# Batches 0 and 1 by head pair: early q and k on the sync queue, transposes on TensorE up front, weights in order on the GpSimd queue

## The chip, the cores and the metric

The kernel runs on one core of a Trainium2 chip. A core has TensorE (PE, with its weight loads PEld), VectorE (DVE), ScalarE (ACT), GpSimd (POOL) and SyncE (SP); each works through its own instructions in their order and waits on semaphores for the others. The metric is the device time of one execution in microseconds (us). The kernel before took 326.36 us, the median of three runs (324.55, 326.36 and 326.54).

## The reference

```python
# q, k, v: (8, 8, 576, 64) float32;  beacon_k, beacon_v: (8, 8, 16, 64)
k_all = concatenate([beacon_k, k], axis=2)
v_all = concatenate([beacon_v, v], axis=2)
scores = matmul(q, k_all.transpose(0, 1, 3, 2)) / sqrt(64)
scores = where(causal, -1e9, scores)          # beacons are always seen, tokens causally
a = softmax(scores)
x = matmul(a, v_all).transpose(0, 2, 1, 3).reshape(4608, 512)
a, b = x @ w1, x @ w2                         # w1, w2: (512, 1024)
out = ((a * b) @ w3) @ w_out                  # w3: (1024, 1024), w_out: (1024, 512)
```

The kernel folds `w3 @ w_out` into one matrix `Wt` (1024 x 512) on the chip and then computes `(a * b) @ Wt`. Inputs and output are float32; all matmuls take float16.

## The kernel before

**Attention.** A batch has eight steps `s`, two for each of the four head pairs `t`. A step is `scores(s)` (matmuls of `kT` and `qT` into two PSUM tiles `ps`, L344), `exps(s, 0)` and `exps(s, 1)` (ACT, L353, into `pT`), `mask(s, j)` (DVE, L365, times the triangles `MA` and `MB`), `values(s)` (matmuls of `pT` and `va` into `pv`, L382), and then a reciprocal and a product on DVE that write `x16` (L390, L391). `va` holds v for one batch in five chunks of 128 keys (beacons first, so the last chunk has 80 rows), with a column of ones for the softmax's sum. `va`, `q16`, `k16`, `qT` and `kT` exist twice; batch `b` uses number `b % 2`. `ps` has two buffers, `pv` one.

**Operands.** `load_q`, `load_k` and `load_v` are DMAs of the GpSimd queue that cast float32 to float16, a chunk of 128 tokens and all heads at a time, in pieces of 64 elements. For batches 0 and 1, `pe_transpose_qk` turns a chunk of q and k by eight TensorE transposes (L210) and two copies out of PSUM (L211 on DVE, L212 on ACT). From batch 2 on, DMA transposes on the sync queue do it (L125, L126).

**Weights.** `w_out` and `w3` come in float32 over the sync queue into staging tiles `st` and are cast by ACT and DVE (`cast`, L150 and L152) into `wo16` and `w3c`. `w1` and `w2` come by casting DMAs of the GpSimd queue into `w12`, behind batch 0's q, k and v (L196).

**The stream of matrix work.** `stream()` yields one matmul of 512 columns at a time. First come the 64 units of `fuse` (L255, each row block of `w3` is first turned by `w3_transposed`, L232, and copied by DVE, L234), then, for each 512 tokens `mc`, 64 units of `ff_ab` (L277) and 32 of `ff_out` (L298). `emit_ff(n)` places the next `n` units between the attention's instructions; `fill[s]` says how many go to step `s`. The order is written out by hand (`manual_schedule`); the framework only adds the semaphore waits which the tiles' reads and writes call for, also between two writes of the same place.

**The start.** TensorE is given 16 units of `fuse`, then batch 0's five chunks of transposes with 8 units behind each of the first four, then `scores(0)` and the steps 0 to 7 with ten units of `fuse`. At `s == 7` come the last six units of `fuse`, `pe_transpose_x(0)` (batch 0's x into `xT`), then 45 units of `ff_ab` between batch 1's five chunks of transposes and three more, then batch 1's steps with 38 units, then `pe_transpose_x(1)`. From batch 2 on (`s >= 16`) a step has 11 or 12 units.

Of the kernel before, what the change touches and what calls it, by code (L numbers as in the profile page):

```python
# [39 lines left out]
def kernel(  # L40
# [21 lines left out]
    NKT = DM // P  # L62
    NFT = DF // P
    NJT = 5
    NB2 = 2
    VS = 72
    scale = float(D**-0.5)
# [17 lines left out]
    sm = ctx.enter_context(tc.tile_pool(name="sm", bufs=4))  # L85
    gp = ctx.enter_context(tc.tile_pool(name="gp", bufs=2))
    wp = ctx.enter_context(tc.tile_pool(name="wp", bufs=2))
    wc = ctx.enter_context(tc.tile_pool(name="wc", bufs=3))
    stg = ctx.enter_context(tc.tile_pool(name="stg", bufs=5))
    asb = ctx.enter_context(tc.tile_pool(name="asb", bufs=3))  # L90
    op = ctx.enter_context(tc.tile_pool(name="op", bufs=4))
    psS = ctx.enter_context(tc.tile_pool(name="psS", bufs=2, space=bass.MemoryType.PSUM))
    psV = ctx.enter_context(tc.tile_pool(name="psV", bufs=1, space=bass.MemoryType.PSUM))
    psM = ctx.enter_context(tc.tile_pool(name="psM", bufs=3, space=bass.MemoryType.PSUM))
# [4 lines left out]
    def load_q(b, c):  # L99
        rows = min(P, S - c * P)  # L100
        nc.gpsimd.dma_start(  # L101
            q16s[b % NB2][:rows, c, :].rearrange("s (h d) -> s h d", h=H),
            q[b, :, ds(c * P, rows), :].rearrange("h s d -> s h d"),
        )
# [11 lines left out]
    def load_k(b, jt):  # L116
        load_kv(b, jt, k, beacon_k, k16s[b % NB2][:, jt, :].rearrange("s (h d) -> s h d", h=H))

    def load_v(b, jt):
        load_kv(b, jt, v, beacon_v, vas[b % NB2][:, jt, :, 0:64])  # L120
# [5 lines left out]
        nc.sync.dma_start_transpose(kTs[i][:, :, ds(c * P, P)], k16s[i][:, c, :])  # L126


    def stage(src):
        st = stg.tile([P, 2 * DM], FP32, name="st")  # L130
        if len(src.shape) == 3:
            nc.sync.dma_start(st.rearrange("p (c n) -> p c n", c=2), src)
        else:
            nc.sync.dma_start(st, src)
        return st

    wo_v = moe_w_out.rearrange("(a c p) n -> a p c n", p=P, c=2)
    srcs = [moe_w3[ts(0, P), :]] + [wo_v[a] for a in range(4)]
    srcs += [moe_w3[ts(kt, P), :] for kt in range(1, NFT)]
    staged = [stage(srcs.pop(0)) for _ in range(5)]  # L140
    w3c = {}

    def cast(engine, row=None, piece=None):
        st = staged.pop(0)
        if row is None:
            dst = wo16[:, ds(2 * piece, 2), :].rearrange("p c n -> p (c n)")
        else:
            w3c[row] = dst = wc.tile([P, 2 * DM], FP16, name="w3c")
        if engine is nc.scalar:
            nc.scalar.copy(dst, st)  # L150
        else:
            nc.vector.tensor_copy(dst, st)  # L152
        if srcs:
            staged.append(stage(srcs.pop(0)))

    nc.vector.memset(ident, 1.0)
    nc.gpsimd.affine_select(
        ident,
        ident,
# [3 lines left out]
        base=0,  # L163
        channel_multiplier=-1,
    )

    for i in range(NB2):
        nc.vector.memset(k16s[i][64:128, 4, :], 0.0)
        nc.vector.memset(vas[i][64:128, 4, :, :], 0.0)
        nc.vector.memset(q16s[i][64:128, 4, :], 0.0)  # L170

    for c in range(NJT):
        load_q(0, c)
        load_k(0, c)
    nc.vector.memset(MA, 1.0)
    nc.vector.memset(MB, 1.0)
    for m, base in (
        (MA[:, 0:128], 0),
        (MA[:, 128:240], Nb),
# [11 lines left out]
        )  # L191
    for c in range(NJT):
        load_v(0, c)
    for c in range(4):
        for i, w in enumerate((moe_w1, moe_w2)):
            nc.gpsimd.dma_start(  # L196
                w12[:, :, ds(i * DF + c * 256, 256)],
                w[:, ts(c, 256)].rearrange("(t p) f -> p t f", p=P),
            )
    for c in range(NJT):  # L200
        load_q(1, c)
        load_k(1, c)


    def pe_transpose_qk(b, c):
        i = b % NB2
        pt = psM.tile([P, 2, NT, P], FP16, name="pm")
        for j, d16 in enumerate((q16s[i], k16s[i])):
            for t in range(NT):
                nc.tensor.transpose(pt[:, j, t, :], d16[:, c, ts(t, P)], ident)  # L210
        nc.vector.tensor_copy(qTs[i][:, :, ts(c, P)], pt[:, 0])  # L211
        nc.scalar.copy(kTs[i][:, :, ts(c, P)], pt[:, 1])  # L212

    def pe_transpose_x(b):
        for i in range(NJT):
            pt = psM.tile([P, NT, P], FP16, name="pm")
            n = QTN[i]
            for t in range(NT):
                nc.tensor.transpose(
                    pt[:, t, 0:n], x16s[b][:n, i, ts(t, P)], ident[:n, :n]  # L220
                )
            dst = xT[:, :, ds(b * S + QT0[i], n)]
            if i % 2:
                nc.scalar.copy(dst, pt[:, :, 0:n])  # L224
            else:
                nc.vector.tensor_copy(dst, pt[:, :, 0:n])


    def w3_transposed(kt):
        pt = psM.tile([P, NFT, P], FP16, name="pm")  # L230
        for rt in range(NFT):
            nc.tensor.transpose(pt[:, rt, :], w3c[kt][:, ts(rt, P)], ident)  # L232
        wT = wp.tile([P, NFT, P], FP16, name="wT")
        nc.vector.tensor_copy(wT, pt)  # L234
        return wT

    cast(nc.scalar, row=0)
    cast(nc.vector, piece=0)
    cast(nc.scalar, piece=1)
    nc.vector.memset(vas[0][:, 0:4, :, 64:65], 1.0)  # L240
    nc.vector.memset(vas[0][0:80, 4, :, 64:65], 1.0)
    cast(nc.vector, piece=2)
    cast(nc.scalar, piece=3)
    cast(nc.vector, row=1)
    nc.vector.memset(vas[1][:, 0:4, :, 64:65], 1.0)
    nc.vector.memset(vas[1][0:80, 4, :, 64:65], 1.0)


    def fuse():
        wT = w3_transposed(0)  # L250
        for kt in range(NFT):
            nxt = w3_transposed(kt + 1) if kt + 1 < NFT else None
            pm = psM.tile([P, DM], FP32, name="pm")
            for rt in range(NFT):
                nc.tensor.matmul(  # L255
                    pm,
                    wT[:, rt, :],
                    wo16[:, rt, :],
                    start=(rt == 0),
                    stop=(rt == NFT - 1),  # L260
                )
                if rt == 0 and kt + 2 < NFT:
                    cast((nc.scalar, nc.vector)[kt % 2], row=kt + 2)
                if rt < NFT - 1:
                    yield
            nc.scalar.copy(Wt[:, kt, :], pm)
            wT = nxt
            yield
# [81 lines left out]
    def exps(s, j):  # L350
        g = 2 * (s % 2) + j
        pT = pTs[s // 2]
        nc.scalar.activation(  # L353
            pT[:, :, ds(GO[g], GW[g])], pss[s][j][:, :, 0 : GW[g]], AF.Exp, scale=scale
        )
# [50 lines left out]
    NSB = 2 * NT  # L406
    NS = B * NSB
    LEFT = 50
    n_second = 38
    n_kept = 10  # L410
    n_first = 96 - n_second - n_kept
    fill = [0] * NS
    fill[0:7] = [2, 2, 2, 1, 1, 1, 1]
    for s in range(NSB, 2 * NSB):
        fill[s] = n_second * (s - NSB + 1) // NSB - n_second * (s - NSB) // NSB
    rest, n = n_kept + 6 * 96 - LEFT, NS - 2 * NSB
    for s in range(2 * NSB, NS):
        fill[s] = rest * (s - 2 * NSB + 1) // n - rest * (s - 2 * NSB) // n

    emit_ff(16)  # L420
    for c in range(NJT):
        pe_transpose_qk(0, c)
        if c < NJT - 1:
            emit_ff(8)
    for c in range(NJT):
        load_v(1, c)
    for c in range(NJT):
        load_q(2, c)
        load_k(2, c)
    scores(0)  # L430
    for j in range(2):
        exps(0, j)
        mask(0, j)
    for s in range(NS):
        b, r = s // NSB, s % NSB
        if s == NSB - 1:
            values(s)
            emit_ff(64 - emitted)
            pe_transpose_x(0)
            for c in range(NJT):  # L440
                emit_ff(n_first // NJT)
                pe_transpose_qk(1, c)
            emit_ff(64 + n_first - emitted)
            scores(s + 1)
            for j in range(2):
                exps(s + 1, j)
                mask(s + 1, j)
            continue
        if s + 1 < NS:
            scores(s + 1)  # L450
            exps(s + 1, 0)
        values(s)
# [50 lines left out]
```

The softmax here doesn't subtract the row's maximum and nothing guards it: scores larger than these inputs give would overflow.

## Time and profile before

| | |
|---|---|
| median of three runs | 326.36 us |
| the profiled execution's own time | 326.37 us |
| its span, first to last instruction | 324.5 us |
| mean granted TensorE clock | 0.995 |
| busy PE / DVE / ACT / POOL | 286.7 / 161.5 / 163.9 / 117.2 us |
| GpSimd's DMA queue (q0) | 119040 packets, 16.52 MB |
| sync's DMA queue (q1) | 53312 packets, 26.75 MB |
| read from HBM, written to it | 39.32 MB, 9.44 MB |

The span ends with TensorE's last matmuls, so what counts in it is the time in which TensorE has nothing to do. Read the table of groups for the duration of one instruction of each kind, the timeline for the times at which stages begin, and the windows for the load of each engine and the bytes per second of a stage. The bytes of a casting DMA are counted as float16, as they land; its source is twice as large. A bracket at the end of a timeline's row is the engine's idle time before it and what ended it.

### The profile page before, as it was taken

To read this page: it belongs to the slowest core of one execution; us is meant where nothing else is said; L and a number is where in the kernel's file an instruction comes from. 1 tells how busy PE (TensorE), PEld (TensorE's weight loads), DVE (VectorE), ACT (ScalarE), POOL (GpSimd) and SP (SyncE) were. 2 spreads that over 40 slices of the span, in tenths; PEclk is the share of its full clock that TensorE was granted. 3 is DMA by queue.
4 is the path that set the end of the run, shared out by engine and by line. 5 is a ranking of instruction groups with operands and counts; after the bars stand their busy time and mean duration, and the time that the engine had idled before them with its cause. 6 is when DMAs were issued, how large, how long until landed. Compare 5 with 4: busy or idle time off the path is not lost.

```text
span 324.5 us, 6919 instructions
## 1 busy us (share of the span) xinstructions
PE 286.7 (88%) x2776; PEld 148.2 (46%) x2776; DVE 161.5 (50%) x375; ACT 163.9 (51%) x229; POOL 117.2 (36%) x153
## 2 busy tenths in 40 slices
PE   1179777987999999999999999799999989999995
PEld 0135445543455445444554455354445544444442
DVE  3324454453664655555654655465555653343342
ACT  2325785467656665655466557464764452230320
POOL 8029869975178019505820960230000000000000
PEclk9997999999999999999999999999999999999999
DMA  8999999999999979999999999996551132202103
GB/s 242 342 288 126 167 175 146 138 144 145 119 113 187 140 86 155 208 138 126 180 176 162 138 206 175 95 146 178 68 84 65 67 32 61 111 2 91 38 2 129
DMA packets 172384, 43.72 MB, mean 135 GB/s; under 512 B 161600, under 2 KB 165696, under 8 KB 172352
## 3 DMA queue, kind: packets, MB, share of 16 engines
q0 software_dynamic: 119040, 16.52, 78.5%
q1 hardware_dynamic: 53312, 26.75, 41.7%
q8 instruction: 22, 0.36, 0.5%
q14 instruction: 10, 0.08, 0.1%
HBM read 39.32 MB, written 9.44 MB: 150 GB/s over the span
## 4 chain that ended last, share of the span: by engine, by line
PE 69%; DMA 12%; ACT 6%; DVE 5%; issue 3%; POOL 3%; DVEq 0%; ACTq 0%; POOLq 0%
PE pm L277 31%; PE pm L298 17%; PE pv L382 10%; PE ps L344 6%; DMA k<-in_beacon_k_dram 6%; ACT pT L353 5%; DMA k<-in_k_dram 3%; PE pm L255 3%; DMA qT<-q 3%; PE pm L210 1%; DVE pT L365 1%; DVE gT L290 1%; DVE x L391 1%; POOL q L101 1%; ACT a_sb L288 1%
## 5 line engine op out<-in xcount | busy, mean ns | idle before, releaser
L277 PE MATMUL pm<-xT,w 128*128 128x512 f16 x576 | 132.8, 379 | 0.6 <-ACT xT L224 0.5
L353 ACT ACTIVATE pT<-ps 128x736 f16<-128x736 f32 (+3 forms) x128 | 105.8, 863 | 35.3 <-PE ps L344 34.5
L288 ACT ACTIVATE a_sb<-pm 128x512 f32<-128x512 f32 x72 | 43.0, 597 | 81.2 <-PE pm L277 80.3
L277 PEld LDWEIGHTS <-w 128*128 128x128 f16 x576 | 53.6, 98 | 58.7 <-issue 0.9
L290 DVE TENSOR_TENSOR gT<-pm,a_sb 128x512 f16<-128x512 f32 x72 | 49.7, 690 | 47.2 <-PE pm L277 43.4
L298 PE MATMUL pm<-Wt,gT 128*128 128x512 f16 x288 | 66.7, 379 | 0.0
L110 POOL DMA_DIRECT2D va<-in_v_dram x40 | 34.0, 871 | 69.2 <-PE pv L382 68.1
L344 PE MATMUL ps<-qT,kT 64*128 64x80 f16 (+3 forms) x704 | 38.3, 228 | 13.0 <-ACT pT L353 9.8
L382 PE MATMUL pv<-va,pT 128*128 128x65 f16 x960 | 41.0, 194 | 3.4 <-DVE pT L365 2.4
L344 PEld LDWEIGHTS <-kT 64*128 64x128 f16 x704 | 20.9, 94 | 42.9 <-issue 41.2
L298 PEld LDWEIGHTS <-gT 128*128 128x128 f16 x288 | 26.9, 98 | 29.6 <-DVE gT L290 0.2
L110 POOL DMA_DIRECT2D k<-in_k_dram x40 | 34.8, 871 | 15.1 <-DMA q<-in_q_dram 10.7
L390 DVE RECIPROCAL rd<-pv 128x4 f32<-128x4 f32 x64 | 12.1, 189 | 55.0 <-PE pv L382 54.9
L101 POOL DMA_DIRECT2D q<-in_q_dram x40 | 35.5, 888 | 10.3 <-DMA k<-in_beacon_k_dram 6.1
L382 PEld LDWEIGHTS <-pT 128*128 128x128 f16 x960 | 33.0, 97 | 13.4 <-DVE pT L365 7.6
L308 DVE TENSOR_SCALAR ot<-pm 128x512 f32<-128x512 f32 x36 | 24.8, 689 | 20.9 <-PE pm L298 20.7
L391 DVE TENSOR_TENSOR x<-pv,rd 128x256 f16<-128x256 f32 x64 | 31.4, 491 | 2.4
L365 DVE TENSOR_TENSOR pT<-pT,MB 128x512 f16<-128x512 f16 x64 | 19.3, 324 | 6.4 <-ACT pT L353 6.4
L255 PE MATMUL pm<-wo,wT 128*128 128x512 f16 x64 | 18.3, 420 | 0.0
L232 PE MATMUL pm<-ident,w3c 128*128 128x128 f16 x64 | 5.8, 243 | 13.6 <-DVE w3c L152 8.3
L365 DVE TENSOR_TENSOR pT<-pT,MA 128x480 f16<-128x480 f16 x32 | 12.7, 398 | 1.8 <-ACT pT L353 1.8
L232 PEld LDWEIGHTS <-w3c 128*128 128x128 f16 x64 | 4.6, 110 | 14.1 <-DVE w3c L152 8.6
(38 smaller groups left out, 82.8 us busy)
## 6 DMA issues: line engine op xcount, KB each, us to landing
out_dram<-ot SPq DMA_DIRECT2D x36, 256.0 KB, 2.4
st<-in_moe_w_dram SPq DMA_DIRECT2D x8, 512.0 KB, 6.7
q<-in_q_dram POOLq DMA_DIRECT2D x32, 128.0 KB, 8.7
k<-in_k_dram POOLq DMA_DIRECT2D x24, 128.0 KB, 9.6
va<-in_v_dram POOLq DMA_DIRECT2D x24, 128.0 KB, 5.5
st<-in_moe_w_out_dram SPq DMA_DIRECT2D x4, 512.0 KB, 7.7
w<-in_moe_w_dram POOLq DMA_DIRECT2D x8, 256.0 KB, 7.9
k<-in_k_dram POOLq DMA_DIRECT2D x8, 112.0 KB, 7.8
```

The lines of the kernel that those rows point to most:

```text
L101: nc.gpsimd.dma_start(q16s[b % NB2][:rows, c, :].rearrange("s (h d) -> s h d", h=H), q[b, :, ds(c * P, rows), :].rearrange("h s d -> s h d"),)
L110: nc.gpsimd.dma_start(dst[ds(p0, rows)], src[b, :, ds(s0, rows), :].rearrange("h s d -> s h d"))
L255: nc.tensor.matmul(pm, wT[:, rt, :], wo16[:, rt, :], start=(rt == 0), stop=(rt == NFT - 1),)
L277: nc.tensor.matmul(pm, w12[:, kt, ds(i * DF + kf * P, P)], xT[:, kt, ds(mc * 512, 512)], start=(kt == 0), stop=(kt == NKT - 1),)
L288: nc.scalar.activation(a_sb, pm, AF.Copy, scale=GS)
L290: nc.vector.tensor_tensor(gT[:, kf, :], pm, a_sb, ALU.mult)
L298: nc.tensor.matmul(pm, gT[:, kf, ts(mt, P)], Wt[:, kf, :], start=(kf == 0), stop=(kf == NFT - 1),)
L344: nc.tensor.matmul(ps[:, hh, ds(col, n)], kT[ds(hh * 64, 64), t, ts(jt, P)], qT[ds(hh * 64, 64), t, ds(q0, n)],)
L353: nc.scalar.activation(pT[:, :, ds(GO[g], GW[g])], pss[s][j][:, :, 0 : GW[g]], AF.Exp, scale=scale)
L365: nc.vector.tensor_tensor(blk, blk, m.unsqueeze(1).to_broadcast([P, 2, n]), ALU.mult)
L382: nc.tensor.matmul(pv[:, 2 * n + hh, 0:65], pT[:, hh, ds(col, P)], va[:, jt, 2 * t + hh, 0:65], start=(jn == 0), stop=(jn == len(BLK[i]) - 1),
L391: nc.vector.tensor_tensor(x16[:, ds(tiles[0], ni), ds(t * P, P)].rearrange("p i (h d) -> p i h d", h=2), pv[:, 0 : 2 * ni, 0:64].rearrange ...
```

## The change

It concerns what happens before batch 2; the code of batches 2 to 7 stays. The pool of `a_sb` goes from three buffers to two, that of `ot` from four to three, and the staging pools `stg` and `wc` go away.

- q and k of batches 0 and 1 are loaded by head pair (`load_pair`), in float32, in runs of six tokens, which are 1536 contiguous bytes: partition `p` holds tokens 6p to 6p+5 of two heads. Batch 0's come over the sync queue, batch 1's over the GpSimd queue. `cast_pair` casts a pair on DVE, `pe_transpose_pair` turns it with 13 transposes (six for q, six for k, one for the beacons) and copies it to `qT` (DVE) and `kT` (ACT), with columns at a distance of six.
- `w_out` and `w3` come by casting DMAs on the GpSimd queue, behind batch 0's v and ahead of `w1` and `w2`; `w3` is kept in a part of `xT` that is written late. The casts on ACT and DVE go.
- Attention comes first: the pairs of batch 0, with `scores(0)`, its exps and its masks between them, and steps 0 to 6 without stream units, but eight at step 6. At `s == 7` come 16 units, `pe_transpose_x(0)`, the other 40 of `fuse`, then 28 units of `ff_ab` (before: 48) between batch 1's four pairs; batch 1's steps have 58 (before: 38).
- `constants(i)` gathers the memsets of `kT`'s unused columns and of `va`'s chunk 4 (rows 64 to 127 to zero) and ones. `constants(0)` stands at the start. `constants(1)` and the memsets of `k16` and `q16` stand behind batch 0's last pair and behind the lines that issue batch 1's loads of v; before, these stood at the start.

```diff
+    def load_pair(b, t):
+        engine = nc.gpsimd if b else nc.sync
+        for i, src in enumerate((q, k)):
+            st = early.tile([P, 2, RUN * D], FP32, name="st")
+            engine.dma_start(
+                st[:NR], src[b, ds(2 * t, 2)].rearrange("h (p j) d -> p h (j d)", j=RUN)
+            )
...
+    def cast_pair(b, t):
...
+            nc.vector.tensor_copy(
+                o16[:NR].rearrange("p j (h d) -> p h j d", h=2),
+                early_qk[b, t, i][:NR].rearrange("p h (j d) -> p h j d", j=RUN),
+            )
...
+    def pe_transpose_pair(b, t):
+        qT, kT = qTs[b % NB2], kTs[b % NB2]
+        for o16, dst, off, copy in (
+            (o16s[t][0], qT, 0, nc.vector.tensor_copy),
+            (o16s[t][1], kT, Nb, nc.scalar.copy),
+        ):
+            pt = psM.tile([P, 1024], FP16, name="pm")
+            for j in range(RUN):
+                nc.tensor.transpose(pt[:, ds(j * NR, NR)], o16[:NR, j, :], ident[:NR, :NR])
...
+            copy(
+                dst[:, t, ds(off, S)].rearrange("p (i j) -> p j i", j=RUN),
+                pt[:, 0:S].rearrange("p (j i) -> p j i", j=RUN),
+            )
...
+    def constants(i):
+        nc.vector.memset(kTs[i][:, :, ds(S + Nb, NJT * P - S - Nb)], 0.0)
+        nc.vector.memset(vas[i][64:128, 4, :, :], 0.0)
+        nc.vector.memset(vas[i][:, 0:4, :, 64:65], 1.0)
+        nc.vector.memset(vas[i][0 : S + Nb - 4 * P, 4, :, 64:65], 1.0)
+
+    constants(0)
+
+    for t in range(NT):
+        load_pair(0, t)
...
     for c in range(NJT):
         load_v(0, c)
+    wo_v = moe_w_out.rearrange("(a c p) n -> a p c n", p=P, c=2)
+    for a in range(4):
+        nc.gpsimd.dma_start(wo16[:, ds(2 * a, 2), :], wo_v[a])
+
+    w316 = xT[:, :, ds(M // 2, 2 * DF)].rearrange("p a (c r) -> p a c r", c=2)
+    for kt in range(NFT):
+        nc.gpsimd.dma_start(w316[:, kt // 2, kt % 2], moe_w3[ts(kt, P), :])
...
-    n_second = 38
+    n_first = 28
     n_kept = 10
-    n_first = 96 - n_second - n_kept
+    n_second = 96 - n_first - n_kept
     fill = [0] * NS
-    fill[0:7] = [2, 2, 2, 1, 1, 1, 1]
+    fill[6] = 8
...
-    emit_ff(16)
-    for c in range(NJT):
-        pe_transpose_qk(0, c)
-        if c < NJT - 1:
-            emit_ff(8)
+    cast_pair(0, 0)
+    pe_transpose_pair(0, 0)
+    cast_pair(0, 1)
+    scores(0)
+    for j in range(2):
+        exps(0, j)
+    pe_transpose_pair(0, 1)
+    cast_pair(0, 2)
+    for j in range(2):
+        mask(0, j)
+    pe_transpose_pair(0, 2)
+    cast_pair(0, 3)
+    pe_transpose_pair(0, 3)
+    for t in range(2):
+        load_pair(1, t)
     for c in range(NJT):
         load_v(1, c)
+    for t in range(2, NT):
+        load_pair(1, t)
+    constants(1)
+    for i in range(NB2):
+        nc.vector.memset(k16s[i][64:128, 4, :], 0.0)
+        nc.vector.memset(q16s[i][64:128, 4, :], 0.0)
     for c in range(NJT):
         load_q(2, c)
         load_k(2, c)
-    scores(0)
-    for j in range(2):
-        exps(0, j)
-        mask(0, j)
...
             values(s)
+            emit_ff(16)
+            pe_transpose_x(0)
             emit_ff(64 - emitted)
-            pe_transpose_x(0)
-            for c in range(NJT):
-                emit_ff(n_first // NJT)
-                pe_transpose_qk(1, c)
+            cast_pair(1, 0)
+            for t in range(NT):
+                emit_ff(n_first // NT)
+                pe_transpose_pair(1, t)
+                if t + 1 < NT:
+                    cast_pair(1, t + 1)
             emit_ff(64 + n_first - emitted)
```

More of the change, by code (lines that the diff above doesn't have):

```diff
@@ L64 @@
     NJT = 5
+    RUN = 6
+    NR = S // RUN
     NB2 = 2
@@ L87 @@
     wp = ctx.enter_context(tc.tile_pool(name="wp", bufs=2))
[L88 to L91, printed above, removed]
+    early = ctx.enter_context(tc.tile_pool(name="early", bufs=8))
+    tiny = ctx.enter_context(tc.tile_pool(name="tiny", bufs=2))
+    bkp = ctx.enter_context(tc.tile_pool(name="bkp", bufs=1))
+    asb = ctx.enter_context(tc.tile_pool(name="asb", bufs=2))
+    op = ctx.enter_context(tc.tile_pool(name="op", bufs=3))
     psS = ctx.enter_context(tc.tile_pool(name="psS", bufs=2, space=bass.MemoryType.PSUM))
@@ L126, in transpose_qk @@
         nc.sync.dma_start_transpose(kTs[i][:, :, ds(c * P, P)], k16s[i][:, c, :])
[L129 to L154, printed above, removed]
@@ L156 @@
-    nc.vector.memset(ident, 1.0)
+    early_qk, early_b = {}, {}
+    def load_pair(b, t):
[5 more added lines that the diff above has]
+            )
+            early_qk[b, t, i] = st
+        if t == 0:
+            bst = bkp.tile([Nb, H, D], FP32, name="bst")
+            engine.dma_start(bst, beacon_k[b].rearrange("h n d -> n h d"))
+            early_b[b] = bst
@@ new lines @@
+    o16s = {}
+    def cast_pair(b, t):
+        if t == 0:
+            b16 = bkp.tile([Nb, DM], FP16, name="b16")
+            nc.vector.tensor_copy(b16, early_b[b].rearrange("p h d -> p (h d)"))
+            early_b[b] = b16
+        o16s[t] = []
+        for i in range(2):
+            o16 = tiny.tile([P, RUN, P], FP16, name=f"o16_{i}")
+            nc.vector.tensor_copy(
+                o16[:NR].rearrange("p j (h d) -> p h j d", h=2),
+                early_qk[b, t, i][:NR].rearrange("p h (j d) -> p h j d", j=RUN),
+            )
+            o16s[t].append(o16)
@@ new lines, in pe_transpose_pair @@
+    def pe_transpose_pair(b, t):
[7 more added lines that the diff above has]
+                nc.tensor.transpose(pt[:, ds(j * NR, NR)], o16[:NR, j, :], ident[:NR, :NR])
+            if off:
+                nc.tensor.transpose(
+                    pt[:, ds(S, Nb)], early_b[b][:, ts(t, P)], ident[:Nb, :Nb]
+                )
+                copy(dst[:, t, 0:Nb], pt[:, ds(S, Nb)])
+            copy(
+                dst[:, t, ds(off, S)].rearrange("p (i j) -> p j i", j=RUN),
+                pt[:, 0:S].rearrange("p (j i) -> p j i", j=RUN),
+            )
@@ new lines, in pe_transpose_x @@
+    def pe_transpose_x(b):
+        for i in range(NJT):
+            pt = psM.tile([P, NT, P], FP16, name="pm")
+            n = QTN[i]
+            for t in range(NT):
+                nc.tensor.transpose(
+                    pt[:, t, 0:n], x16s[b][:n, i, ts(t, P)], ident[:n, :n]
+                )
+            dst = xT[:, :, ds(b * S + QT0[i], n)]
+            if i % 2:
+                nc.scalar.copy(dst, pt[:, :, 0:n])
+            else:
+                nc.vector.tensor_copy(dst, pt[:, :, 0:n])
@@ L157 @@
+    nc.vector.memset(ident, 1.0)
+    nc.vector.memset(MA, 1.0)
+    nc.vector.memset(MB, 1.0)
+    def constants(i):
[6 more added lines that the diff above has]
+        load_pair(0, t)
     nc.gpsimd.affine_select(
@@ L165 @@
     )
[L167 to L170, printed above, removed]
-    for c in range(NJT):
[L173 to L176, printed above, removed]
     for m, base in (
@@ L199, with w3_transposed @@
             )
-    for c in range(NJT):
[L201 to L246, printed above, removed]
-    def fuse():
+    def fuse():
+        def w3_transposed(kt):
+            pt = psM.tile([P, NFT, P], FP16, name="pm")
+            for rt in range(NFT):
+                nc.tensor.transpose(pt[:, rt, :], w316[:, kt // 2, kt % 2, ts(rt, P)], ident)
+            wT = wp.tile([P, NFT, P], FP16, name="wT")
+            nc.vector.tensor_copy(wT, pt)
+            return wT
         wT = w3_transposed(0)
@@ L261, in fuse @@
                 )
-                if rt == 0 and kt + 2 < NFT:
-                    cast((nc.scalar, nc.vector)[kt % 2], row=kt + 2)
                 if rt < NFT - 1:
@@ L418 @@
         fill[s] = rest * (s - 2 * NSB + 1) // n - rest * (s - 2 * NSB) // n
-    emit_ff(16)
-    for c in range(NJT):
-        pe_transpose_qk(0, c)
-        if c < NJT - 1:
-            emit_ff(8)
+    cast_pair(0, 0)
[13 more added lines that the diff above has]
+        load_pair(1, t)
     for c in range(NJT):
         load_v(1, c)
+    for t in range(2, NT):
[4 more added lines that the diff above has]
+        nc.vector.memset(q16s[i][64:128, 4, :], 0.0)
     for c in range(NJT):
@@ L437 @@
             values(s)
+            emit_ff(16)
+            pe_transpose_x(0)
             emit_ff(64 - emitted)
-            pe_transpose_x(0)
-            for c in range(NJT):
-                emit_ff(n_first // NJT)
-                pe_transpose_qk(1, c)
+            cast_pair(1, 0)
+            for t in range(NT):
+                emit_ff(n_first // NT)
+                pe_transpose_pair(1, t)
+                if t + 1 < NT:
+                    cast_pair(1, t + 1)
             emit_ff(64 + n_first - emitted)
```

## The prediction

> **What bounds the kernel now.** I read the slices of the span first, for where TensorE stands idle:
>
> ```profile
> PE   1179777987999999999999999799999989999995
> DVE  3324454453664655555654655465555653343342
> DMA  8999999999999979999999999996551132202103
> ```
>
> A slice is 8.1 us. From about 90 us on TensorE is nearly full to the end, so time can only be won or lost before; there the DMA row is full while PE reads 1, 1, 7, 9, 7, 7, 7. The windows by stage, cut where the timeline of TensorE shows the first instruction of each stage, say how long each takes (columns: stretch, length, busy us and instructions of PE, PEld, DVE, ACT, POOL; clock, DMA share, GB/s as landed):
>
> ```profile
> 2.00:16.00 14.00, 2.36 (x18) 1.82 (x19) 4.58 (x15) 3.79 (x5) 6.48 (x8) 1.00 1.18 329
> 24.00:31.00 7.00, 7.00 (x51) 4.09 (x49) 3.32 (x7) 3.30 (x6) 6.99 (x12) 0.76 1.92 123
> 35.66:53.06 17.40, 12.35 (x229) 7.68 (x228) 9.09 (x28) 14.06 (x19) 13.27 (x18) 1.00 1.89 170
> 53.06:56.33 3.27, 2.51 (x27) 1.64 (x26) 1.88 (x5) 1.66 (x3) 3.27 (x5) 1.00 2.21 139
> 56.33:69.22 12.89, 12.84 (x88) 6.81 (x88) 5.48 (x10) 5.71 (x11) 11.71 (x15) 1.00 1.98 144
> 69.22:93.47 24.25, 19.40 (x277) 10.95 (x276) 13.31 (x36) 16.82 (x23) 11.50 (x15) 1.00 1.57 129
> 93.47:265.58 172.11, 165.21 (x1767) 84.75 (x1766) 95.51 (x232) 100.71 (x139) 56.59 (x71) 1.00 1.32 134
> ```
>
> The first row is the load of q, k and weights; the second casting DMAs of 64 elements alone on the queue. Then batch 0's steps, the rest of `fuse` with batch 0's x, the stage between the batches, batch 1's steps, and batches 2 to 7. Batch 0's steps are ACT's (14.06 of 17.40 us). The queue itself is priced by the GpSimd timeline, where each issue waits until an earlier transfer has landed:
>
> ```profile
> 40.46 0.89 POOL L101 DMA_DIRECT2D q<-in_q_dram  x1 [0.84 <-DMA w<-in_moe_w_dram]
> 41.78 0.88 POOL L110 DMA_DIRECT2D k<-in_k_dram  x1 [0.43 <-DMA w<-in_moe_w_dram]
> 43.11 0.87 POOL L101 DMA_DIRECT2D q<-in_q_dram  x1 [0.45 <-DMA w<-in_moe_w_dram]
> 44.45 0.87 POOL L110 DMA_DIRECT2D k<-in_k_dram  x1 [0.47 <-DMA w<-in_moe_w_dram]
> ```
>
> One weight transfer of 128 x 1024 elements lands every 1.33 us (0.52 MB of float32, so 394 GB/s read). Last, DVE's timeline for two prices:
>
> ```profile
> 1.46 0.30 DVE L169 MEMSET va<- 64x288 uint32 x1
> 13.93 0.69 DVE L152 CAST w3c<-st 128x1024 f16<-128x1024 f32 x1 [2.45 <-DMA st<-in_moe_w_dram]
> ```
>
> Today the memset of `va`'s chunk 4 runs at 1.46 us, long before the load that writes rows 0 to 79 of the same chunk.
>
> **The change, part by part.** The part that decides is the smallest. In the built program of the changed kernel DVE's instructions stand in this order:
>
> ```
> qT<-pm        batch 0, pair 3
> Memset kT_1
> Memset va_1 64x288        [waits for a GpSimd DMA]
> Memset va_1 (ones) x2, k16 and q16 x4
> Reciprocal rd<-pv, x16<-pv,rd      step 0
> pT<-pT,MB x2                       step 1
> ```
>
> `constants(1)` stands behind `load_v(1, c)`, and both write chunk 4 of `va_1`, rows 64 to 79. So the memset waits for that load to land. It is the 37th DMA of the GpSimd queue: 6 for v of batch 0, 4 for `w_out`, 8 for `w3`, 8 for `w1` and `w2`, 5 for pairs 0 and 1 of batch 1 and the beacons, then 6 for v of batch 1. DVE works in order, so step 0's reciprocal and step 1's masks queue behind the memset. TensorE then waits in `values(1)` for these masks with steps 2 to 7 and the whole stream behind it, and ACT stops once step 2's exps are done, as `scores(3)` stands behind `values(1)`.
>
> When does that load land? Up to it 2.39 MB (q, k of batch 0, sync), 0.61 MB as landed (v), 20 weight transfers, 1.21 MB (pairs) and 0.61 MB (v) pass. The first bytes move at about 2 us. (2.39 + 0.61) MB at 329 GB/s are 9.1 us; 20 x 1.33 = 26.6; 1.21 MB at 329 is 3.7; 0.61 MB at the second row's 123 GB/s is 5.0; from last byte to semaphore I take 1.6 us, estimated from the output stores (2.4 us to landing less 0.8 for 256 KB at 329). T = 2.0 + 9.1 + 26.6 + 3.7 + 5.0 + 1.6 = 48.0 us. From below: all 16.5 MB of float32 at 394 GB/s, 41.9 + 3.6 = 45.5. From above: the weights at the pace of today's staged loads, whose casts start at 4.20 and, four transfers later, at 12.49, so 2.07 us each beside another queue: 20 x 0.74 more, 62.8. I take 48, since the 1.33 us row is the same queue, cast and size.
>
> The trace reads 394 GB/s through that queue. [...]
>
> From T on, by rows of today:
> - DVE: memsets 0.30 + 0.09 + 0.07 + 4 x 0.27 = 1.5, reciprocal and product 0.18 + 0.42, two masks 0.56: `values(1)` starts at T + 2.7 = 50.7 (today 40.40).
> - From there to the end of `values(7)` today 12.7 us (to 53.06), with eight units woven in. Now also eight, but in one place (step 6), with two `w3` transposes and a copy of 0.69 ahead of them: 13.0, between 12 and 15. End 63.7.
> - 56 units of `fuse` x 0.216 (379 ns a matmul, overlapped; 1.94 us for nine in the chain) = 12.1, six groups of `w3` transposes x 0.46 = 2.8, batch 0's x 2.1 (54.19 to 56.33): 17.0, against 3.3 today. By now all weights are in. End 80.7, today 56.33.
> - Between the batches 28 units instead of 48: 6.1, and 52 transposes at 0.055 (0.45 for eight) = 2.9. DVE has two casts of 768 elements (0.69 x 768/1024 = 0.52 each), a strided copy of 576 between 0.47 and 0.78 (the copies of 512 from PSUM took 0.42 in f16, 0.69 in f32) and a `gT` of 0.69 for each pair: 2.4 x 4 = 9.7. I take 10, between 9 and 12. End 90.7, today 69.22.
> - Batch 1's steps have 58 units instead of 38, 4.3 us more, with 4.85 us of idle PE in that row: between 24.3 and 28.6. A step of batches 2 to 7 takes 172.1 / 48 = 3.59 us for 11.2 units, so 1.17 beside them; 8 x (1.17 + 7.25 x 0.216) = 21.9, and today's start of the stage (2.5) and batch 1's x (2.0) make 26.4. End 117.1, today 93.47: 23.6 us late.
>
> What is saved lies in front of T and is lost in the wait: the idle TensorE up to 20 us, the ACT and DVE casts of the weights (1.04 and 0.69 each), and some 7,700 packets of 64 elements on the GpSimd queue, which does not set the end after 93 us. The smaller pools cost nothing while the first store of four has landed when the fourth `ot` is written: with today's times the tightest is issued at 125.13, lands 2.4 later at 127.5, and the fourth `ot` starts at 128.06. Without that cover it would be a few tenths for each of six `mc`. Batches 2 to 7 are the same instructions, so I carry the lateness to the end.
>
> **Sum.** Span 324.5 + 23.6 = 348.1; what lies around the span was 1.9 (own time 326.37, equal to the median of 326.36): 350 us.
>
> **The rivals.**
> - *The weights land slowly.* `w3` goes in rows of 1024, `w_out` in rows of 512, and no row shows these as casting DMAs; at 2.07 us each T is 62.8 and the time 350 + 14.8 = 365. For it: the staged loads' pace; against: those shared the engines with 64-element packets.
> - *DVE isn't held* (other side): the load is in before DVE comes to the memset. Then batch 0 goes on as soon as pair 3 is there: q and k landed at 2.0 + 9.1 + 1.6 = 12.7, casts, copies and step 1's exps about 4 us: `values(1)` at 17 instead of 50.7, the last row of `w3` at 11.1 + 12 x 1.33 + 1.6 = 28.7 in time for `fuse` at 30, so 33.7 us less: 316. Against it: over 15 MB stand ahead of that load; it decides only if the load lands before T = 48.0 - 23.6 = 24.4 us, 16.5 MB in 22 us or 737 GB/s, against 394 in the trace.
> - *The lateness is partly caught up*: the stage between the batches takes 9 us and batch 1's extra units vanish in its idle 4.85 us: 350 - 1 - 2.1 = 347, and with T = 45.5, 344.5.
>
> **How the numbers follow.** The forecast with its bounds has 0.83 (0.15 of it the third rival, which ends inside them), the slow weights 0.12, DVE not held 0.04, no change 0.01. The range goes from 344 (T = 45.5 and the catch-up) to 363 (most of the way to the slow weights). The three runs of before lie within 0.6%, so about 1% can be told from no change: faster 0.04, within 1% 0.01, slower 0.95.
>
> **What would show it.** In the profile after: the memset of `va` 64x288 on DVE with some 30 us of idle before it, released by DMA `va`; PE with next to nothing in slices 3 to 6; `values(1)` at about 51 us, `scores(17)` at about 117; batches 2 to 7 again 172 us. The forecast is wrong if that memset runs before 25 us, or if weight transfers land at a pace other than 1.33 us.

## The result

The changed kernel takes 366.79 us (median of four runs, 365.29 to 369.64), the kernel before 325.46 us beside it: 1.128 times as long, with a 95% interval of 1.120 to 1.137. The direction was forecast, the size was not: 350 us with a range of 344 to 363. The profiled execution took 365.29 us, with a span of 363.3.

The slices of the span after (9.1 us each) show where it went:

```profile
PE   1430008798769999996999999998999999999995
DVE  4820024535855565553455646554655464334333
DMA  9999999499000099999989999999944112210203
```

TensorE reads 0, 0, 0 from 27 to 55 us while the DMA row is full. What ends that hole is the second of these rows of DVE's timeline:

```profile
20.09 0.14 DVE L201 MEMSET kT<- 128x96 uint32 x1
51.73 0.30 DVE L202 MEMSET va<- 64x288 uint32 x1 [31.50 <-DMA va<-in_v_dram]
53.53 0.18 DVE L397 RECIPROCAL rd<-pv 128x4 f32<-128x4 f32 x1
```

The memset of `va_1` waited 31.5 us for the load of v. Step 0's reciprocal, whose matmuls had ended at 19.84 us, came right behind the memsets. Because this memset runs after the load, it also leaves zeros in v of batch 1's last 16 tokens: the changed kernel computes batch 1 without them. TensorE waited for the same thing, as the list of who waited for whom says:

```profile
PE pv L389 <- DVE x L398: 31.4, 1, 31.4
```

The stages by window (stretch, length, busy us and instructions of PE, PEld, DVE, ACT, POOL; clock, DMA share, GB/s):

```profile
2.00:12.00 10.00, 3.15 (x33) 2.32 (x33) 4.88 (x10) 3.59 (x5) 7.92 (x10) 1.00 1.19 251
12.00:16.00 4.00, 1.48 (x16) 1.12 (x14) 4.00 (x5) 2.94 (x5) 2.30 (x4) 1.00 2.15 169
54.23:70.56 16.33, 12.82 (x200) 9.17 (x200) 8.20 (x25) 8.50 (x11) 4.91 (x6) 1.00 1.37 117
70.56:86.89 16.33, 15.97 (x125) 9.13 (x122) 7.44 (x14) 4.59 (x8) 14.41 (x17) 1.00 1.91 139
86.89:100.93 14.04, 9.91 (x81) 5.30 (x79) 11.06 (x13) 9.44 (x11) 0.00 (x0) 1.00 0.20 13
100.93:131.06 30.13, 25.60 (x296) 13.25 (x296) 16.01 (x39) 19.46 (x26) 3.24 (x5) 0.94 0.11 20
131.06:363.30 232.24, 220.07 (x2020) 109.33 (x2018) 118.53 (x266) 112.57 (x159) 56.00 (x70) 1.00 1.02 115
```

| step of the sum | forecast, us | measured, us | difference |
|---|---|---|---|
| the load lands and the memset runs (T) | 48.0 | 51.7 | +3.7 |
| from there to `values(1)` | 2.7 | 2.5 | -0.2 |
| `values(1)` to the end of `values(7)` | 13.0 | 16.3 | +3.3 |
| the rest of `fuse`, batch 0's x | 17.0 | 16.3 | -0.7 |
| between the batches | 10.0 | 14.0 | +4.0 |
| batch 1 to `scores(17)` | 26.4 | 30.1 | +3.7 |
| batches 2 to 7, to the end | 231.0 | 232.2 | +1.2 |

These add up to 15 us, which is the difference of the spans (348.1 forecast, 363.3). The rest of the miss is that the profiled execution lies 1.5 us under the median.

### The profile page after: what moved, and what is told of

The parts are those of the page before. It is cut to its first block, busy times and chain, and to the rows that moved or that the text cites. A ratio compares the mean times of both kernels' runs of the same rounds, so it can differ in the third digit from the quotient of the medians.

```text
span 363.3 us, 6960 instructions
## 1 busy us (share of the span) xinstructions
PE 292.6 (81%) x2800; PEld 152.0 (42%) x2800; DVE 177.2 (49%) x387; ACT 169.1 (47%) x229; POOL 114.0 (31%) x152
## 4 chain that ended last, share of the span: by engine, by line
PE 54%; DMA 23%; DVE 6%; POOL 5%; ACT 5%; issue 4%; SPq 1%; DVEq 0%; POOLq 0%
PE pm L284 24%; PE pm L305 12%; PE pv L389 8%; DMA k<-in_k_dram 6%; PE ps L351 5%; DMA va<-in_v_dram 4%; DMA qT<-q 4%; PE pm L264 4%; ACT pT L360 3%; DMA st<-in_k_dram 3%; DMA w<-in_moe_w_dram 3%; DMA xT<-in_moe_w_dram 2%; POOL va L113 2%; DMA out_dram<-ot 2%; DVE gT L297 1%
## 5 line engine op out<-in xcount | busy, mean ns | idle before, releaser
L284 PE MATMUL pm<-xT,w 128*128 128x512 f16 x576 | 134.3, 381 | 5.0 <-DVE qT L177 3.8
L389 PE MATMUL pv<-va,pT 128*128 128x65 f16 x960 | 42.8, 197 | 36.3 <-DVE x L398 31.4
L389 PEld LDWEIGHTS <-pT 128*128 128x128 f16 x960 | 34.4, 99 | 47.2 <-DVE x L398 32.5
L351 PE MATMUL ps<-qT,kT 64*128 64x80 f16 (+3 forms) x704 | 40.7, 238 | 13.5 <-ACT pT L360 9.5
L351 PEld LDWEIGHTS <-kT 64*128 64x128 f16 x704 | 21.9, 98 | 42.1 <-issue 38.0
L113 POOL DMA_DIRECT2D k<-in_k_dram x30 | 26.6, 886 | 3.4 <-DMA q<-in_q_dram 1.3
L104 POOL DMA_DIRECT2D q<-in_q_dram x30 | 26.1, 871 | 2.1 <-issue 0.8
L177 DVE COPY qT<-pm 128x576 f16<-128x576 f16 x8 | 16.6, 2072 | 6.0 <-PE pm L171 6.0
L177 ACT COPY kT<-pm 128x576 f16<-128x576 f16 x8 | 16.6, 2080 | 0.0
L171 PE MATMUL pm<-ident,o 96*128 96x96 f16 x96 | 7.4, 242 | 10.9 <-DVE o L157 10.5
L202 DVE MEMSET va<- 64x288 uint32 x2 | 0.6, 298 | 31.6 <-DMA va<-in_v_dram 31.5
```

Source lines behind the costliest of these rows:

```text
L104: nc.gpsimd.dma_start(q16s[b % NB2][:rows, c, :].rearrange("s (h d) -> s h d", h=H), q[b, :, ds(c * P, rows), :].rearrange("h s d -> s h d"),)
L113: nc.gpsimd.dma_start(dst[ds(p0, rows)], src[b, :, ds(s0, rows), :].rearrange("h s d -> s h d"))
L177: copy(dst[:, t, ds(off, S)].rearrange("p (i j) -> p j i", j=RUN), pt[:, 0:S].rearrange("p (j i) -> p j i", j=RUN),)
L284: nc.tensor.matmul(pm, w12[:, kt, ds(i * DF + kf * P, P)], xT[:, kt, ds(mc * 512, 512)], start=(kt == 0), stop=(kt == NKT - 1),)
L351: nc.tensor.matmul(ps[:, hh, ds(col, n)], kT[ds(hh * 64, 64), t, ts(jt, P)], qT[ds(hh * 64, 64), t, ds(q0, n)],)
L389: nc.tensor.matmul(pv[:, 2 * n + hh, 0:65], pT[:, hh, ds(col, P)], va[:, jt, 2 * t + hh, 0:65], start=(jn == 0), stop=(jn == len(BLK[i]) - 1),
```

## The experiments

**Form of the experiments.** All of them replace the DMA transposes of batches 2 to 7 by plain copies of the same tiles, so what these batches compute is not turned; what is compared is what comes before batch 2. Their base is p0_after_plain, and the kernel before in the same form is p4_before_plain. Up to batch 2 the code is that of the two kernels, word for word, but for the edit shown.

**The base.**

```diff
-        nc.sync.dma_start_transpose(qTs[i][:, :, ds(c * P, rows)], q16s[i][:rows, c, :])
+        nc.sync.dma_start(qTs[i][:, :, ds(c * P, rows)],
+            q16s[i][:, c, :].rearrange("p (t n) -> p t n", t=NT)[:, :, 0:rows])
...  (k and x likewise)
```

> The changed kernel as a base for the experiments: the DMA transposes of batches 2 to 7 (q, k and x) are replaced by plain copies of the same tiles on the same queue, behind the same waits, so that what batches 2 to 7 compute is not turned. Up to batch 2 nothing is touched. If the transposes don't set the time of batches 2 to 7, 366.8 us again, between 362 and 370, with the memset of va at about 51.7 us; if they do, batches 2 to 7 take less than 228 us instead of 232.

363.08 us (362.80 to 364.75); the memset of `va` ran at 52.9 us, 1.2 later than in the changed kernel, whose code up to there is the same. From `scores(17)` to the end it took 228.5 us (134.23 to 362.7) instead of 232.2. The transposes are worth some 4 us in batches 2 to 7, and the loss stands.

**The kernel before in this form**, run twice on different occasions:

> The kernel before with its DMA transposes of batches 2 to 7 replaced by plain copies, as in the base (what these batches compute is not turned). It is what the experiments of this form are to be compared with. The changed kernel lost 3.7 us by that replacement, so 325.5 - 3.7 = 322 us, between 319 and 326; then the run with both edits (322.1) is level with it.

> The kernel before in the same form once more, to be compared with the run of 16 units on the same chip: 321, between 320 and 322.5. The run of 16 units should be below it by 0.5 to 1.2%.

320.99 and 321.31 us. In this form the change costs 42 us.

**The wait, taken away.**

```diff
     constants(0)
+    constants(1)
...
-    constants(1)
     for i in range(NB2):
         nc.vector.memset(k16s[i][64:128, 4, :], 0.0)
```

> The base with one line moved: constants(1) stands behind constants(0), at the start, instead of behind the loads of v of batch 1. Theory 1 (DVE is held by the load until 51.7 us, and this is most of the loss): DVE goes on at about 21 us, values(1) starts at 22 to 24 us instead of 54.2, and 31 us come back: base - 31 = 336 us, between 331 and 340, so still about 3% slower than before, since the slow copies of 2.07 us and the longer stage between the batches remain. Rival (the start is bound by the queue anyway: the weights or batch 1's pairs arrive too late, and what the wait gives back is lost in front of fuse or between the batches): above 350 us.

332.75 us, 30.3 less than the base: theory 1. Step 1's reciprocal, which follows `values(1)`, first in the base and then in this run:

```profile
57.17 0.20 DVE L403 RECIPROCAL rd<-pv 128x6 f32<-128x6 f32 x1 [1.34 <-PE pv L395]
```

```profile
24.29 0.20 DVE L404 RECIPROCAL rd<-pv 128x6 f32<-128x6 f32 x1 [1.81 <-PE pv L396]
```

Of these 33 us nearly all arrive at the end. The rival is out: neither weights nor pairs were late enough to matter. What is left is still 12 us slower than the kernel before in this form. (The memset now comes before the load, so v of batch 1 is whole.)

**The wait alone, put into the kernel before.**

```diff
-        nc.vector.memset(vas[i][64:128, 4, :, :], 0.0)
+        if i == 0:
+            nc.vector.memset(vas[i][64:128, 4, :, :], 0.0)
...
     for c in range(NJT):
         load_v(1, c)
+    nc.vector.memset(vas[1][64:128, 4, :, :], 0.0)
```

> The run before with one memset moved: va of batch 1, chunk 4, rows 64 to 127, is set to zero behind the lines that load v of batch 1 (so the last 16 tokens' v of batch 1 are zero, as in the changed kernel). Theory 1: DVE stops behind the last copy of batch 0's q and waits for that load, which is issued at 53.7 us and lands about 4.5 us later, at 58; the first mask, and with it values(0), moves from 38.7 to about 59, so 20 us more than the run before, between 16 and 24. Rival (a wait of DVE is absorbed by the stream's work on TensorE and by ACT): under 6 us more.

344.94 us, 24 more than p4_before_plain, at the top of what was expected. Step 0's reciprocal is at 57.6 us instead of 36.2, so 21 of the 24 us are there when the wait ends; the granted clock, 0.57 from 34 to 60 us, is low mainly while TensorE waits. DVE's timeline of this run has the same picture in a kernel that is otherwise the old one:

```profile
56.25 0.30 DVE L435 MEMSET va<- 64x288 uint32 x1 [22.91 <-DMA va<-in_v_dram]
56.58 0.41 DVE L372 TENSOR_TENSOR pT<-pT,MA 128x480 f16<-128x480 f16 x1
```

**The copies out of PSUM.**

```diff
-                dst[:, t, ds(off, S)].rearrange("p (i j) -> p j i", j=RUN),
-                pt[:, 0:S].rearrange("p (j i) -> p j i", j=RUN),
+                dst[:, t, ds(off, S)].rearrange("p (i j) -> p i j", j=RUN),
+                pt[:, 0:S].rearrange("p (j i) -> p i j", j=RUN),
```

> The base, with the copies of pe_transpose_pair walked in the other order: writes to qT and kT are contiguous, and the reads from PSUM have the stride. The wait stays. Theory 2 (it is the writes at a distance of 12 bytes that cost 2.07 us a copy, and these copies make the stage between the batches 4 us longer than forecast and batch 1's first step 1.7 us longer): a copy falls to 0.6 to 0.8 us on DVE and ACT, the stage from 14.0 to about 10 us, the time from 366.8 to about 360, between 358 and 362. Rival (the stride costs the same on the side of the reads, or the copies are covered): a copy stays near 2 us and the time above 364.

356.61 us, 6.5 less than the base; the 358 to 362 expected were counted from 366.8, and the size of the step, 6.8 us to 360, is right: theory 2. The groups of the stage between the batches, first of the changed kernel, then of this one (busy us, mean ns):

```profile
L177 DVE COPY qT<-pm 128x576 f16<-128x576 f16 x4 | 8.3, 2074 | 4.0 <-PE pm L171 4.0
L177 ACT COPY kT<-pm 128x576 f16<-128x576 f16 x3 | 6.3, 2084 | 0.0
```

```profile
L183 DVE COPY qT<-pm 128x576 f16<-128x576 f16 x4 | 3.0, 758 | 4.3 <-PE pm L177 4.3
L183 ACT COPY kT<-pm 128x576 f16<-128x576 f16 x4 | 2.6, 645 | 0.0
```

The same 576 elements take 2.07 us on either engine when they are written at a distance of 12 bytes, and 0.76 us on DVE and 0.65 on ACT when the distance is on the side of the reads. (Copies of 512 contiguous elements out of PSUM took 0.42 and 0.59 us before, which makes an estimated 0.48 and 0.66 for 576: the distance still costs some 0.3 us on DVE's reads, and nothing on ACT's.) The stage falls from 14.0 to 10.4 us (87.90 to 98.26), and batch 1 to `scores(17)` from 30.1 to 27.2.

Not all of the 3.0 us in batch 1 are the copies' own. Up to the first seven units it gains 1.4 us, because the first exps no longer stand behind the last slow copy on ACT. The other 1.6 us are in these units and what follows them up to the next seven, first in the changed kernel, then in this run, each with its window, in which the granted clock (the third number from the end) reads 0.55 and 1.00:

```profile
105.23 2.92 PE L284 MATMUL pm<-xT,w 128*128 128x512 f16 x7
105.20:108.20 3.00, 3.00 (x17) 0.95 (x16) 1.78 (x5) 0.93 (x2) 0.00 (x0) 0.55 0.00 0
```

```profile
101.21 1.68 PE L290 MATMUL pm<-xT,w 128*128 128x512 f16 x7
101.20:104.20 3.00, 3.00 (x46) 1.71 (x43) 1.78 (x5) 1.70 (x3) 0.00 (x0) 1.00 0.00 0
```

These seven units are slow in every trace with the slow copies (3.17 us in the base and in p1_const_first), but also in two of the five with fast ones (2.75 us in p6_woven and 2.79 in p10_pools, both below). What lowers the clock there is not shown.

**Both.**

> The base with both edits: constants(1) at the start and copies with contiguous writes. If the two are separate terms of the sum, 336 less 6 to 7 for the stage between the batches and batch 1, less 3 to 5 more at the start, where four pairs of copies now lie in the chain to values(1): 326, between 320 and 330, so near the kernel before. If the queue binds (rival of the run with the constants alone), above 345.

322.13 us (ratio to the kernel before 0.993, interval 0.988 to 0.998; p4_before_plain has 0.991, 0.987 to 0.995). The two are separate terms: 30.3 and 6.5, and 4.1 more because four pairs of copies now stand in the chain to `values(1)`, as expected: it starts at 18.37 us instead of 22.75 in p1_const_first. With both gone the change is level with the kernel before, and no better.

**The block of eight units.**

```diff
-    fill[6] = 8
+    fill[3:7] = [2, 2, 2, 2]
```

> The run with both edits, and the eight units of step 6 dealt out as two each in steps 3 to 6, where the weights are just in (wo from 19 us, the first rows of w3 at 23 to 25). Theory 3 (the forecast's 13 us from values(1) to the end of values(7) were 3.3 short because the eight units, two groups of transposes and a copy of 0.69 stand in one block between step 6 and values(7): 5.4 us from step 6's reciprocal to step 7's, against 1.9 before): the gap falls to 2 to 3 us, the others grow by 0.2 or so each, and 2 to 3 us come back: 319.5, between 318 and 321. Rival (TensorE runs at half pace in these steps, 1.56 us for 24 matmuls of pv against 0.90, and that is the term): the units cost the same wherever they stand, 322 +- 1.

320.35 us (ratio 0.992, 0.988 to 0.996): the intervals overlap with the run of both edits, so the times don't tell the two apart. The traces show part of the 2 to 3 us that were expected. From step 6's reciprocal to step 7's the time fell from 5.4 to 2.6 us, as said, but from step 3's to step 4's it rose from 1.7 to 3.4, where the first two groups of transposes and the copy that they wait for now stand; step 7 comes 1.1 us earlier. (The profiled executions are equally long all the same, 319.8 and 319.6 us: this one met the low clock in batch 1.) The rival is right in its fact, and its price is small. TensorE's timeline of the run of both edits, in whose steps 1 to 5 no unit stands,

```profile
22.48 1.56 PE L396 MATMUL pv<-va,pT 128*128 128x65 f16 x24
26.66 1.56 PE L396 MATMUL pv<-va,pT 128*128 128x65 f16 x24
```

and of this one, in which the units begin at 25.9 us:

```profile
22.64 1.56 PE L396 MATMUL pv<-va,pT 128*128 128x65 f16 x24
29.02 0.90 PE L396 MATMUL pv<-va,pT 128*128 128x65 f16 x24
```

So TensorE does run at little over half pace (1.56 us against 0.90 for 24 matmuls) for a long stretch of attention alone. It isn't the units that end this: in the changed kernel the same 24 matmuls took 1.56 us at 58.57 and 1.07 at 62.52, and its first unit begins at 64.98. The price of the slow pace is small: from step 3's reciprocal to step 6's 5.7 us in the run of both edits, slow almost throughout, against 5.0 in the changed kernel, which is fast from 61.3 us (60.17 to 65.19).

**Why T was late: the shape of the load.** In the changed kernel's GpSimd timeline the second `w_out` transfer, by the order of the waits, landed at

```profile
19.02 0.54 POOL L242 DMA_DIRECT2D xT<-in_moe_w_dram  x1 [0.53 <-DMA wo<-in_moe_w_out_dram]
```

where the forecast had 11.1 + 2 x 1.33 + 1.6 = 15.4: all of the 3.7 us is in by then. The windows show two parts of it. From 2 to 12 us, while q and k load, 251 GB/s landed instead of 329. Then q and k are in, and what is left of v, in packets of 64 elements, comes alone. The packets from 13 to 14 us:

```profile
DMA packets 1211, 0.15 MB, mean 153 GB/s; under 512 B 1211, under 2 KB 1211, under 8 KB 1211
```

So of the 3.0 MB, 2.5 MB took 10 us instead of the 7.6 that 329 GB/s would give, and the other 0.5 MB some 3 instead of 1.5: an estimated 2.4 and 1.5 us too much. Three runs took the first part, the load of q and k, apart: larger pieces on fewer partitions, the same pieces on more partitions, and no other queue beside it.

```diff
-    RUN = 6
+    RUN = 9          # 64 partitions; gT, a_sb and ot with one buffer
```

> The base with runs of nine tokens instead of six: pieces of 2304 bytes on 64 partitions instead of 1536 on 96, as many bytes. To make room, gT, a_sb and ot have one buffer, so that only the first 55 us are read. Theory 4 (the forecast's T was 3.7 us short because pieces of 1536 bytes pass at about 220 GB/s, where the staged loads of before, in pieces of 2 and 4 KB, gave 310): the bytes per second from 2 to 12 us rise from 249 to between 270 and 300, the weights land 1 to 2 us earlier, and the memset of va starts 1 to 2 us earlier than in the base (52.9). Rival (the 64-element packets of v beside it set the pace): no change beyond 0.5 us.

```diff
                 st[:NR], src[b, ds(2 * t, 2)].rearrange("h (p j) d -> p h (j d)", j=RUN)
+            ) if b else engine.dma_start(
+                st.rearrange("p h n -> p (h n)")[:, 0 : 9 * D],
+                src[b, ds(2 * t, 2)].rearrange("h (p j) d -> (h p) (j d)", j=9),
             )
...  (batch 0's casts read 96 of these partitions, so tokens lie in other places)
```

> The base, with q and k of batch 0 loaded into 128 partitions in pieces of 2304 bytes (partition h x 64 + i takes nine tokens of head h), as many bytes in as many DMAs; the casts read what lies there, so batch 0 computes with tokens in the wrong places. Theory 5 (the rate of the sync queue goes with the number of partitions that a DMA writes: 302, 234 and 172 GB/s from 2 to 10 us at 128, 96 and 64 partitions): the sync queue moves about 300 GB/s from 2 to 10 us (2.3 MB or all of it), and the memset of va starts 2 to 4 us earlier than in the base (52.9). Rival (it is the small packets beside it, or 2304-byte pieces are slow as such, 172 in the run with nine tokens): 240 GB/s or less, and the memset within 1 us of 52.9.

```diff
     cast_pair(0, 3)
+    nc.vector.memset(MB, 1.0)
+    ...  (MB's triangles and all loads of the GpSimd queue follow here)
```

> The base, in which the GpSimd queue starts only behind the casts of batch 0's last pair (the triangle MB, which it has to fill in first, is set to one by DVE there), so that batch 0's q and k have the DMA engines to themselves. Only the first 12 us are read. Theory 5 (partitions): alone, 96 partitions still move no more than 250 GB/s on the sync queue from 2 to 10 us. Rival (the packets of v beside it take the rest): 290 to 320 GB/s.

What the sync queue moved from 2 to 8 us (packets, MB, share of 16 engines' time), one line each from the kernel before (128 partitions, pieces of 2 and 4 KB), the changed kernel (96, 1536 bytes), p7_run9 (64, 2304 bytes), p8_128 (128, 2304 bytes) and p9_alone (96, 1536 bytes, nothing beside it):

```profile
q1 hardware_dynamic: 816, 1.81, 91.8%
```

```profile
q1 hardware_dynamic: 1125, 1.44, 91.6%
```

```profile
q1 hardware_dynamic: 632, 1.05, 79.4%
```

```profile
q1 hardware_dynamic: 870, 1.53, 81.7%
```

```profile
q1 hardware_dynamic: 1170, 1.50, 105.6%
```

In six microseconds these are 302, 240, 175, 255 and 250 GB/s. What theory 4 expected did not come: with larger pieces, but on 64 partitions, the load was slower, and the memset of `va` came at 56.9 us instead of 52.9. The rivals with the small packets beside it fell: without them the queue moved 250 GB/s instead of 240. At the same piece of 2304 bytes, 128 partitions instead of 64 gave 255 instead of 175. So in these runs the number of partitions that the load writes counts. How much of the step from 302 to 240 it makes is not shown: no run has 96 and 128 partitions with the same piece, and 128 partitions gave 255, under the 302 which theory 5 had expected. With them the memset came at 50.5 us, 2.4 earlier than in the base but 1.2 earlier than in the changed kernel. (Only the start of p7_run9 and p9_alone is of use; their 419 and 374.5 us carry later losses. p8_128 took 361.75 us in one run.)

**The pools.**

```diff
-    asb = ctx.enter_context(tc.tile_pool(name="asb", bufs=2))
-    op = ctx.enter_context(tc.tile_pool(name="op", bufs=3))
+    asb = ctx.enter_context(tc.tile_pool(name="asb", bufs=3))
+    op = ctx.enter_context(tc.tile_pool(name="op", bufs=4))      # on p6_woven; early: 7
```

> The run with both edits and the units dealt out, with a_sb and ot back at three and four buffers as before, and seven instead of eight buffers for the early tiles to make room (the last load of batch 0's k then starts a little later). Read from step 16's reciprocal to step 63's: 168.3 us in the run of before in this form, 169.9 in this one without the edit. If the pools cost these 1.6 us: 168.3, and the time about 319. If not: 169.9 and 320 to 321.

319.27 us in two runs (ratio 0.986, 0.962 to 1.009: unclear). Step 16 to step 63 took 168.7 us, against 169.9 without the edit and 168.3 in p4_before_plain. The other traces in this form agree: with the smaller pools (the base, p1, p2, p3, p6, p8 and p9) this stretch took 169.1 to 172.4 us, in five of the seven 169.8 to 170.0; with the larger ones (p4, p4b, p5, p10 and the next run) 168.3 to 168.7. So the smaller pools cost some 1.5 us, though the times of this pair alone don't tell it.

**One step further.**

```diff
-    fill[3:7] = [2, 2, 2, 2]
+    fill[3:7] = [4, 4, 4, 4]         # on p10_pools
```

> The run with both edits, dealt-out units and the larger pools, with four units instead of two in each of steps 3 to 6 (16 in all). If these steps are ACT's and TensorE is warm in them, eight units more (1.7 us of TensorE) go into its idle time there, less one group of transposes and its copy: 1 to 1.5 us less than 319.3, so 318. Rival (the copies of the turned rows on DVE get in the way of the masks): 319 to 320.

318.85 us (ratio 0.985, 0.981 to 0.989) against p4b_before_plain's 321.31 on the same chip (0.990, 0.987 to 0.994). That is 0.8% less, within what was expected against that run, but the intervals overlap; of the 1 to 1.5 us expected against the run of the pools, 0.4 came. So no form of the change was shown to beat the kernel before clearly. It is a statement on the start alone, since in these runs batches 2 to 7 aren't turned.

## Why the prediction was wrong

*The mechanism was right.* The memset behind the 37th DMA, DVE's queue behind the memset, `values(1)` and with it TensorE behind DVE: all at the places named, and the largest single term. p1 gives back 30.3 us by moving it, p5 makes 24 us of it in the other kernel. The rival of a DVE that isn't held did not happen; but its 316 us was badly off too: with the wait away the time is 332.75 us, even in the form without transposes, and 10.6 of these go only with the slow copies (322.13 with both edits).

*Three terms of the sum were mis-sized, all in the same direction, so nothing cancelled.*
1. **The copies of `qT` and `kT`**, put at 0.47 to 0.78 us from copies of 512 contiguous elements: 2.07 us each. The forecast took the element count from the rows and left out that the writes have a distance of 12 bytes, which no row of before has. p2 measures the term: 6.5 us, by the stages 3.7 between the batches and 3.0 in batch 1. Of the latter 1.4 are the first exps' wait behind the last copy on ACT, and 1.6 a stretch at a granted clock of 0.55, which the forecast did not have and which is not shown to be the copies' work. The bound from above should have been drawn much wider for a form of access that the trace doesn't show.
2. **The first term of T**, 9.1 us for q, k and v at 329 GB/s: 3.7 us too short. That is the rate of today's staged loads, into 128 partitions in pieces of 2 and 4 KB. q and k came into 96 in pieces of 1536 bytes, and 251 GB/s landed. And 0.61 MB of v were priced at 329 here, where the same sum prices batch 1's v, as many bytes in the same small packets, at 123; what was left of it when q and k were in went at 153. The weights went as forecast: from the second `w_out` transfer (19.02) to the last of `w12` (the issue that waited for it runs at 42.77) 18 transfers took 23.75 us, 1.32 each against 1.33. The last part, pairs and v, took 9.0 (to 51.73) against 8.7.
3. **`values(1)` to `values(7)`**, 13.0 us for 16.3: the forecast saw that the eight units stand in one place, behind two groups of transposes and a copy, but added only 0.3 us for it to today's 12.7, in which they are woven in. In one block they stand on the path: 5.4 us from step 6 to step 7 against 1.9 before. p6 shows that dealing them out moves part of that and gives back 1.1 us.

Batch 1's remaining 0.8 us (27.2 against 26.4 with fast copies) and the 1.2 us of the last batches are small; the forecast called the pools free, and the traces around p10 put most of the latter down to them.

*The range* of 344 to 363 was made from T's bounds, from a catch-up that did not come, and at the top from slow weights, which did not come either. It held no case in which the new instructions, rather than the wait, were dearer than the nearest rows. Even the stages' own upper bounds, 15, 12 and 28.6 us, were not added to its top, and all three were passed: 16.3, 14.0 and 30.1.

## What to carry to other kernels

When an initialisation is moved behind a load that writes the same tile, the framework orders them, and an in-order engine then holds everything behind it until that load lands, here DVE for 31.5 us behind the 37th DMA of the GpSimd queue: count the load's place in its queue. An access pattern that no row of the trace shows, here writes at a distance of a few bytes, isn't priced by its element count (2.07 us here, where contiguous writes are an estimated 0.48 on DVE); put the stride on the side of the reads (0.76 us on DVE and 0.65 on ACT here), or bound it by several times the contiguous row. And a load's rate is taken from a row with the same number of partitions and the same packets (here 175 GB/s into 64 partitions and 255 into 128 with the same pieces, and 153 for packets of 64 elements alone); where there is none, it gets a bound of its own.

## What was not expected of the hardware

- DVE and ACT take the same 2.07 us for 576 float16 elements written at a distance of 12 bytes (3.6 ns an element). In p7_run9, at 18 bytes, it was 2.68 us on DVE; with contiguous writes and reads from PSUM at a distance of 192 bytes, 0.76 us on DVE and 0.65 on ACT. Why the distance costs this much is not shown.
- In attention alone TensorE took 1.56 us for 24 matmuls that take 0.90 us elsewhere, while the granted clock of these stretches reads 1.00. (Elsewhere the column does move: 0.55 where seven units took 2.92 us instead of 1.68.) The pace, 0.58, is not in the clock column, and in the run of both edits it lasted from 15.5 to 29.4 us, with TensorE 87% busy from 15.5 to 29.6 by the profile: what set it and what ended it is not shown.
- A load's rate on the sync queue from HBM went from 175 to 255 GB/s when the same bytes, in the same pieces, were written to 128 partitions instead of 64 (p7_run9 and p8_128, one run each).
